# Gated linear attention and a max-of-three feed-forward: a new order of the pieces on five engine queues

## Chip, cores, metric

The kernel runs on one core of a Trainium2 chip. The metric is the device time of one execution in microseconds (us). The engines are TensorE (PE in the profile, its weight loads PEld), VectorE (DVE), ScalarE (ACT), GpSimd (POOL) and SyncE (SP), which here only issues transfers.

## The reference

Two stages, joined by a change of layout. `B, H, S, D = 4, 8, 768, 48`; the second stage has 3072 tokens, model width 384 and hidden width 768.

```python
for t in range(S):
    state = alpha[:, :, t, :, None] * state + einsum('bhd,bhe->bhde', k[:, :, t], v[:, :, t])
    y[:, :, t] = einsum('bhd,bhde->bhe', q[:, :, t], state)
x = y.transpose(0, 2, 1, 3).reshape(B * S, H * D)
h = maximum(maximum(x @ w1, x @ w2), x @ w3)
out = h @ w_out
```

## The kernel before

The recurrence is computed in chunks. A step `s` (0 to 11) is one batch element and 256 tokens; step `s` needs the state that step `s - 4` left. Three weights are needed for one maximum, so the kernel uses max(x w1, x w2, x w3) = x w1 + max(x (w2 - w1), x (w3 - w1), 0): two products per hidden column through `wdif`, and x (w1 w_out) is added in the last product through `w1o`.

Nothing is ordered by loops. `ORDER` is a string of pieces, and `emit` issues them from left to right; each engine runs its own instructions strictly in that order and waits by semaphores for what they need. A piece such as `k0p@5` is letter, index, engine (`v` DVE, `a` ACT, `p` POOL, none for TensorE or SP), step; `#6,4` gives it PSUM banks. One engine's late piece thus holds all its later ones. The letters:

- Loads and stores, all on SP's one queue: `l0` to `l3` load a (alpha), k, q, v of a step into rings of four buffers (L102); `K` loads a third of a weight, part of it into ring buffers of steps 2 and 3 (L118, L121); `J` loads the small constants `ca` and `cb` (L130); `W` stores 128 rows of the output (L500); `D` transposes q and k of a step by DMA (L290), from step 5 on, in two halves.
- Decays: `m` multiplies pairs of alpha (L205); `N` and `r` are logarithms and inverses on ACT (L209, L214, L216); `u` and `w` scale k and q of the nearer token (L219, L222); `c` sums the logarithms on TensorE (L231, L234), one long and four short matmuls; `e`, `f`, `g` are its exponentials on ACT (L240, L250); `k` and `q` scale k and q by them (L260).
- Attention: `T` transposes on TensorE for steps 0 to 4 (L283) and `t` copies the result out; `A` makes scores, 32 small matmuls (L304), and `a` masks them on DVE (L319; L315 for step 0); `V` scales v (L168) and `v` spreads it in two copies; `Y` with even index adds the chunk's part of the output (16 small matmuls, 64 for step 0), with odd index the state's part (12) (L330); `x` copies the result out for the next stage.
- State: `S` makes its update on TensorE (L388), `s` adds it (L400), `M` and `z` decay it (L377, L404), `y` spreads it in two copies.
- Feed-forward: `d` makes the weight differences (L418); `b`, `B`, `n`, `C`, `P`, `p` make `w1o`; `G` is a group of six matmuls of 256 columns (L452), six groups a step; `h` takes the maximum (odd index: always DVE, L461; even: DVE L463 or ACT L465); `O` is the last product (L486), `o` scales it out of PSUM (L168, L170).
- `H` is `warm`: matmuls on a blank tile whose result is not used (L505). `H2^t1@0` waits first for a piece's result (L524). They stand only in the first part.

So a step is: load, decays, `k` and `q`, transposes, `A`, `a`, `Y`, `x`, `G`, `h`, `O`, `o`, `W`; and steps overlap as the string has them.

Of the kernel before, what the change touches and what calls it, by code (L numbers as in the profile page):

```python
# [23 lines left out]
def kernel(  # L24
# [513 lines left out]
    def emit(order):  # L538
# [12 lines left out]
        l0@0 m0v@0 r0a@0 N0a@0 r1a@0 J1@0 l1@0 u0v@0 H15@0#0 c0@0#0 e0a@0 k0v@0 K0@0 b0a@0 f0a@0 J0@0 I0a@0
        H5@0#1 B0@0#1 l2@0 w0v@0 g0a@0 q0v@0 H6@0#2 T0@0#2 M0p@0 l0@1 m0p@1 r0a@1 N0a@1 K2@0 d1v@0 H3@0#3 c0@1#3
        e0a@1 g0a@1 K1@0 d0p@0 r1a@1 T1@0#4 t1v@0 t0a@0 H3@0#5 H2^t1@0#5 A1@0#5,6 l1@1 u0v@1 k0v@1 l2@1 w0v@1
        f0a@1 q0v@1 A0@0#7,0 a0v@0 a2v@0 a1v@0 l3@0 a3v@0 n0a@0 V0a@0 l3@1 V0a@1 v1p@1 v0p@1 K3@0 H5@0#4
        S0@0#4,2 T0@1#3 t0a@1 T1@1#7 t1a@1 H2@0#5 S0@1#5,0 b1a@0 s0v@1 s0a@0 l0@2 m0v@2 N0a@2 K4@0 H1@0#6
        A0@1#6,1 a0v@1 a1v@1 A1@1#3,7 a3v@1 M0p@1 z0p@1 y0a@1 a2v@1 z0p@0 d2p@0 y0a@0 B1@0#5 n1v@0 K5@0 d3v@0
        s1v@0 l0@4 m0v@4 l2@2 c0@2#4 l1@2 g0a@2 M0p@2 Y0@0#6,1 x0a@0 Y3@0 x1a@0 K7@0 K6@0 r0a@2 r1a@2 w0p@2
        Y2@1#7 Y3@1 x1a@1 s1v@1 f0a@2 d4p@0 G1@0#3 N0a@4 l3@2 K8@0 d5p@0 Y0@1#5 u0v@2 e0a@2 q0v@2 G0@0#2 h0a@0
        x0a@1 k0v@2 G2@0#6 G3@0#1 h2a@0 h3v@0 c0@4#7 e0a@4 g0a@4 h1v@0 f0a@4 G2@1#0 h2a@1 G0@1#4 T0@2#2 t0v@2
        T1@2#5 t1v@2 K10@0 l1@4 h0a@1 b2a@0 G1@1#6 h1v@1 K11@0 K9@0 G3@1#1 l0@3 V0a@2 r0a@4 v1a@2 A1@2#3,7 a2v@2  # L560
        A0@2#0,2 a0v@2 a3v@2 S0@2#5,4 s0a@2 a1v@2 B2@0#6 n2v@0 G4@1#3 G4@0#0 G5@1#7 l0@5 z0p@2 l2@4 h3v@1 v0a@2
        Y0@2#5 x0v@2 Y2@2#2 y0a@2 Y3@2 x1a@2 M1p@0 u0p@4 k0v@4 G5@0#6 h4a@0 h5v@0 G5@2#1 l1@3 C2a@0 C0v@0 l2@3
        G4@2#5 l3@3 r1a@4 C1a@0 h4v@2 z1p@0 y1a@0 G0@2#2 m0v@3 s1v@2 h4a@1 G2@2#0 h2v@2 h5v@1 h5v@2 h0a@2 P0@0#6
        P1@0#5 N0a@3 r0a@3 p1a@0 w0v@4 q0v@4 c0@3#4 P2@0#3 e0a@3 m0p@5 G1@2#0 M0p@4 N0a@5 c0@5#7 f0a@3 r0a@5
        r1a@3 p0a@0 u0v@3 k0p@3 p2a@0 G3@2#1 h3v@2 f0a@5 T0@4#2 t0v@4 g0a@5 e0a@5 g0a@3 l3@4 T1@4#5 t1v@4 O0@0#6
        l0@7 l0@6 A1@4#3,1 h1v@2 V0a@3 a2v@4 M0p@5 w0p@3 q0v@3 A0@4#2,7 o0a@0 l1@5 S0@3#4,5 s0a@3 M1p@1 M0v@3
        z0p@3 l1@6 l2@5 O1@0#0 a1v@4 r1a@5 V0a@4 a3v@4 s1v@3 T0@3#3 t0v@3 o1a@0 T1@3#6 t1a@3 z1p@1 O0@1#4 m0p@7
        a0v@4 o0v@1 l0@8 y0a@3 N0a@7 A1@3#7,1 A0@3#5,3 l3@5 v0a@3 S0@4#0,6 W0@0 s0v@4 a1v@3 a0v@3 a2v@3 v0p@4
        m0p@6 N0a@6 O0@2#2 v1a@3 y1a@1 w0v@5 o0a@2 z0p@4 u0p@5 s1v@4 c0@7#4 v1p@4 c0@6#0 O1@1#3 r0a@7 o1a@1
        g0a@7 l0@9 g0a@6 Y3@3#5 a3v@3 Y2@3 Y0@3#7 r0a@8 x0a@3 Y0@4#2 Y2@4#6 l1@7 y0p@4 Y1@4 Y3@4 x1v@4 x0v@4  # L570
        O1@2#3 o1v@2 m0v@8 k0v@5 f0a@6 W1@0 l2@6 G0@4#1 h0v@4 e0a@6 x1a@3 M0p@6 G4@3#7 h4v@3 G2@3#6 G1@3#2
        G3@3#3 h2v@3 h3v@3 G4@4#1 l3@7 W0@2 q0p@5 D0@5 V0a@5 f0a@7 M1p@2 v1a@5 r1a@8 r0a@6 u0p@6 N0a@8 m0p@9
        r1a@6 c0@8#0 G0@3#5 e0a@8 h0a@3 r1a@7 h1v@3 G5@3#7 h5v@3 w0p@6 k0p@6 q0v@6 l3@6 D1@5 G5@4#6 G3@4#3 N0a@9
        V0a@7 h4a@4 h5v@4 e0a@7 c0@9#5 f0a@9 e0a@9 M1p@3 g0a@8 u0p@7 G2@4#2 h2a@4 f0a@8 g0a@9 M0p@8 G1@4#7 h1v@4
        O0@3#1 z1v@2 y1a@2 h3v@4 S0@5#6,4 s0v@5 k0p@7 r0a@9 A0@5#2,0 a1v@5 D1@6 W0@1 D0@6 z0v@5 A1@5#5,7 a2v@5
        a3v@5 o0a@3 V0a@6 l2@7 W0@3 O1@3#3 a0v@5 o1v@3 O1@4#6 y0a@5 o1a@4 r1a@9 v0p@7 v0p@5 Y0@5#0 Y1@5 v0v@6
        s1v@5 x0v@5 Y2@5#5 Y3@5 x1a@5 l0@10 S0@7#7,1 M1p@4 M0p@7 z1p@3 s0v@7 z0p@7 W1@1 l3@8 A1@6#2,3 a2v@6
        a3v@6 A0@6#6,4 a1v@6 S0@6#0,5 s0v@6 G2@5#7 G3@5#2 h2a@5 h3v@5 a0v@6 y0a@7 w0p@7 M1p@5 q0p@7 l1@8 D0@7
        D1@7 l2@8 G4@5#3 h4a@5 G1@5#4 G0@5#0 h0v@5 m0p@10 N0a@10 y1p@3 M0p@9 G5@5#7 O0@4#2 o0a@4 z1p@4 z0p@6
        y0a@6 c0@10#6 e0a@10 f0a@10 h1v@5 h5v@5 O1@5#3 O0@5#0 v1v@7 v1v@6 Y2@6#2 l0@11 s1v@6 u0v@8 k0v@8 g0a@10  # L580
        M1v@6 M0v@10 V0a@8 o1a@5 v0v@8 Y3@6 x1v@6 Y1@6#4 Y0@6 l2@9 r0a@10 S0@8#7 A0@7#5,6 s1v@7 a1v@7 s0v@8
        A1@7#3,2 a3v@7 a0v@7 a2v@7 x0a@6 G2@6#1 h2a@6 G3@6#6 h3v@6 G5@6#7 W1@3 G0@6#2 h0v@6 w0p@8 y1a@4 m0p@11
        z0p@8 N0a@11 W0@4 Y3@7#5 Y2@7 x1v@7 l1@9 W1@2 l3@9 Y0@7#3 Y1@7 x0a@7 c0@11#4 e0a@11 q0p@8 D0@8 D1@8
        g0a@11 r0a@11 w0p@9 M1p@7 l1@10 y0v@8 q0p@9 G1@6#1 h1v@6 G4@6#6 h4a@6 f0a@11 h5v@6 u0v@9 o0a@5 V0a@9
        v0a@9 z1p@5 k0p@9 D0@9 y1a@5 G0@7#2 G5@7#5 G1@7#3 r1a@11 h0v@7 z1p@6 h1v@7 z1p@7 u0p@10 k0p@10 G2@7#1
        G3@7#6 G4@7#4 h4v@7 l3@10 h2v@7 h5v@7 h3v@7 O0@6#7 o0a@6 O1@6#0 D1@9 A0@8#2,3 a0v@8 A1@8#4,1 a2v@8 o1v@6
        a3v@8 v1a@8 V0a@10 S0@9#5 s0v@9 a1v@8 O0@7#6 O1@7#7 v1v@9 z0v@9 Y3@8#2 Y2@8 x1a@8 y0p@9 Y1@8#4 Y0@8
        x0a@8 r1a@10 l2@10 w0p@10 q0p@10 l2@11 w0p@11 S0@10#0 s0v@10 A1@9#1,5 a2v@9 A0@9#3,2 a1v@9 a3v@9 l1@11
        a0v@9 v0a@10 G4@8#4 G0@8#0 h0v@8 G2@8#1 h2v@8 G5@8#2 h4a@8 h5v@8 Y2@9#5 Y0@9#3 l3@11 Y1@9 x0v@9 Y3@9
        y1a@6 G3@8#0 G1@8#1 h3v@8 x1a@9 G0@9#4 h0a@9 u0v@11 G2@9#2 q0v@11 G4@9#3 h1v@8 G5@9#0 D1@10 k0p@11  # L590
        G3@9#5 h2a@9 h3v@9 G1@9#4 D0@10 h4a@9 V0a@11 y1v@7 h5v@9 h1v@9 z0v@10 W1@4 o0a@7 O0@8#1 A0@10#2,5
        A1@10#3,0 a2v@10 a0v@10 a3v@10 D1@11 D0@11 v1v@11 S0@11#4 s0v@11 W0@7 a1v@10 O1@9#6 v1v@10 W1@6 O0@9#3
        o1a@9 W1@9 W0@5 o0a@9 W0@9 A1@11#2,0 a2v@11 a3v@11 A0@11#4,5 W0@6 v0p@11 M0p@11 W1@5 O1@8#6 y0p@10
        Y3@10#3 Y2@10 a0v@11 x1a@10 z0p@11 Y1@10#2 a1v@11 Y0@10 x0a@10 Y1@11#0 y0p@11 Y0@11 x0v@11 Y2@11#4 Y3@11
        o1a@7 W1@7 G3@10#3 x1a@11 G0@10#5 G2@10#2 o0v@8 G1@10#0 h0v@10 G4@10#7 h1v@10 h2a@10 h3v@10 G4@11#4
# [40 lines left out]
```

## Time and profile before

| | |
|---|---|
| runs | 143.85, 144.14, 146.13 us (median 144.14) |
| profiled execution | 143.54 us, its span 141.8 us |
| busy | PE 93%, DVE 80%, ACT 67%, POOL 52% of the span |
| mean granted TensorE clock | 0.988 |
| moved by DMA | 32.42 MB, 229 GB/s on average |
| a load of 384 KB | 5.3 us from issue to landing (median) |
| first, last matmul | 1.19 us; the last begins at 137.99 and ends at 138.3 us |

The span runs from the first to the last instruction; the execution's time is 1.74 us longer. A row of the timeline has start, duration, engine, line, operation and tiles, and in brackets the engine's idle time before it and what ended that. A row of waits has the engine and its line, what it waited for, and total, number and longest. SPq is SP's queue. A row of the table by stages has the stretch, its length, each engine's busy time with its instructions, the granted clock, the DMA engines' share and the rate. Some times in the prediction are of single pieces: the string and the trace were laid side by side, engine by engine. The landing of a transfer is the last of its 16 engines' records.

### The profile page before, as it was taken

How to read it: one execution, taken by the hardware profiler on the slowest of the kernel's cores; microseconds unless marked ns; L12 is line 12 of the kernel's file. 1: busy time of each engine (PE TensorE's matmuls, PEld its weight loads, DVE VectorE, ACT ScalarE, POOL GpSimd, SP SyncE). 2: the span in 40 equal slices, each digit the busy share in tenths (PEclk: the TensorE clock that was granted, in tenths of full speed). 3: DMA queues.
4: the chain of work that ended last, by engine and by line, in shares of the span. 5: the costliest groups of instructions: out<-in, count | busy, mean ns of one | idle time of the engine just before them, and what ended most of it. 6: DMA issues, size and time to landing. Idle time of an engine off the chain costs nothing.

```text
span 141.8 us, 5323 instructions
## 1 busy us (share of the span) xinstructions
PE 132.4 (93%) x2236; PEld 96.6 (68%) x2236; DVE 113.7 (80%) x215; ACT 95.5 (67%) x202; POOL 73.8 (52%) x107
## 2 busy tenths in 40 slices
...
GB/s 107 312 344 325 306 332 269 277 333 361 263 271 249 282 310 253 322 201 109 219 204 274 254 190 332 320 143 182 202 260 199 196 112 161 244 97 16 96 72 150
DMA packets 73031, 32.42 MB, mean 229 GB/s; under 512 B 65456, under 2 KB 73008, under 8 KB 73008
## 3 DMA queue, kind: packets, MB, share of 16 engines
...
q8 instruction: 17, 0.28, 0.8%
...
## 4 chain that ended last, share of the span: by engine, by line
PE 75%; SPq 8%; DVE 7%; DMA 4%; ACT 2%; issue 2%; DVEq 0%
PE bank L452 32%; PE bank L486 23%; PE bank L330 8%; SPq L102 5%; DMA rv<-in_v_dram 4%; PE bank L304 4%; PE bank L388 2%; SPq L118 2%; PE bank L440 2%; PE bank L283 2%; DVE lat L319 1%; DVE hT L461 1%; ACT qkT L162 1%; DVE qk L260 1%; PE bank L231 1%
## 5 line engine op out<-in xcount | busy, mean ns | idle before, releaser
L452 PE MATMUL bank<-xT,wdif 128*128 128x256 f16 x432 | 50.8, 275 | 0.8 <-DVE h L463 0.8
L452 PEld LDWEIGHTS <-wdif 128*128 128x128 f16 x432 | 41.4, 98 | 6.8 <-issue 1.1
L319 DVE TENSOR_TENSOR lat<-bank,cb 128x512 f16<-128x512 f32 x44 | 28.0, 681 | 1.3 <-PE bank L304 1.2
L461 DVE TENSOR_TENSOR hT<-bank,h 128x512 f16<-128x512 f32 x36 | 23.9, 685 | 6.2 <-PE bank L452 3.2
L486 PE MATMUL bank<-wo,hT 128*128 128x384 f16 (+1 forms) x150 | 27.5, 320 | 0.0
L486 PEld LDWEIGHTS <-hT 128*128 128x128 f16 x150 | 14.5, 98 | 8.9
L168 ACT ACTIVATE ob<-bank,ca 128x384 f32<-128x384 f32 (+1 forms) x18 | 10.3, 570 | 14.2 <-PE bank L486 12.9
L465 ACT ACTIVATE h<-bank 128x512 f16<-128x512 f32 x21 | 12.2, 599 | 8.1 <-PE bank L452 7.8
L486 PE MATMUL bank<-w1o,xT 128*128 128x384 f16 (+1 forms) x75 | 15.9, 321 | 0.0
L260 POOL TENSOR_TENSOR qk<-rk,ic 128x768 f16<-128x768 f32 x6 | 11.5, 1920 | 4.7 <-DVE rk L219 3.3
L505 PE MATMUL bank<-hT 128*128 128x512 f16 x42 | 12.7, 440 | 1.4 <-DVE hT L603 1.2
L168 ACT ACTIVATE vt<-rv,ca 128x768 f16<-128x768 f32 x12 | 11.3, 945 | 3.2 <-DMA rv<-in_v_dram 3.2
L162 ACT CAST xT<-bank 128x384 f16<-128x384 f32 x16 | 7.5, 480 | 7.1 <-PE bank L330 7.1
L222 POOL TENSOR_TENSOR rq<-rq,ic 128x384 f32<-128x384 f32 x8 | 8.0, 999 | 7.4 <-DMA rq<-in_q_dram 4.3
L463 DVE TENSOR_SCALAR h<-bank 128x512 f16<-128x512 f32 x15 | 9.9, 680 | 1.2 <-PE bank L452 1.2
L164 POOL COPY vu<-vt 64x384 f16<-64x384 f16 x14 | 7.3, 520 | 5.2 <-ACT vt L168 4.7
L205 POOL TENSOR_TENSOR ra<-ra 128x384 f32<-128x384 f32 x7 | 7.5, 1075 | 3.3 <-DMA ra<-in_alpha_dram 3.2
L162 ACT CAST st<-kept 64x192 f16<-64x192 f32 x26 | 9.0, 347 | 0.3
L260 POOL TENSOR_TENSOR qk<-rq,ac 128x768 f16<-128x768 f32 x5 | 9.1, 1814 | 0.1
L330 PE MATMUL bank<-lat,vu 128*32 128x128 f16 x352 | 8.3, 224 | 0.8 <-issue 0.7
L486 PEld LDWEIGHTS <-xT 128*128 128x128 f16 x75 | 6.5, 98 | 3.1
L505 PEld LDWEIGHTS <-hT 128*128 128x128 f16 x42 | 4.2, 110 | 6.4 <-issue 3.2
...
## 6 DMA issues: line engine op xcount, KB each, us to landing
...
```

Of the source, the lines that this page charges most:

```text
L162: nc.scalar.copy(out=dst, in_=src)
L168: nc.scalar.mul(dst, src, col)
L222: engines[eng].tensor_mul(raw("q", s, 0), raw("q", s, 0), decays["k"][s % 3][:, 0])
L260: engines[eng].tensor_mul(dst, src, by)
L319: nc.vector.tensor_mul(lats[s % 2][u][:, i], bank(("aps", s, u, i), [HP, P]), pmask.unsqueeze(1).broadcast_to([P, HP, P]))
L330: nc.tensor.matmul(y[x][C * m:C * (m + 1), f, :], lhs, rhs, start=(s, x, m) not in begun, stop=(seen[x] or U * (s // B) + x == 0) and n == ...
L452: nc.tensor.matmul(gps[:, j, :], wdif[:, f, g, jj * P:(jj + 1) * P], xT[:, f].rearrange("p u t -> p (u t)"), start=(f == 0), stop=(f == NF ...
L461: nc.vector.tensor_max(hTs[s % NH][:, 2 * jg:2 * jg + 2, :], gps, h)
L463: nc.vector.tensor_scalar_max(h, gps, 0.0)
L465: nc.scalar.activation(out=h, in_=gps, func=AFT.Relu)
L486: nc.tensor.matmul(ops, lhs, (w1o if what == "x" else wo16)[:, j, cols], start=((what, j) == every[0]), stop=((what, j) == every[-1]))
L505: nc.tensor.matmul(wps, blank[:, :P], blank, start=True, stop=True)
```

## The change

Only `ORDER` is replaced. The pieces stay the same but for the `H` fills; their sequence on every engine's queue, the PSUM banks, and the engine of a number of pieces change: `q` on POOL 5 to 9 and on DVE 7 to 3, `u` the same; gates `M` on POOL 17 to 9, on DVE 3 to 11; even `h` on ACT 21 to 26; `o` on ACT 18 to 13, on DVE 7 to 12; one to three pieces each of `b`, `d`, `k`, `m`, `n`, `p`, `s`, `v`, `x`, `y`, `z`, `V`. The transposes stay as they were: steps 0 to 4 on TensorE, 5 to 11 by DMA. The new order comes from a search over a plan whose costs were altered: longer two-part copies (`v`, `y`), dearer small constants (`J`), and TensorE held when a packet of its instructions is asked for late.

The start, the parts around steps 5 and 6, and the end:

```diff
-        l0@0 m0v@0 r0a@0 N0a@0 r1a@0 J1@0 l1@0 u0v@0 H15@0#0 c0@0#0 e0a@0 k0v@0 K0@0 b0a@0 f0a@0 J0@0 I0a@0
-        H5@0#1 B0@0#1 l2@0 w0v@0 g0a@0 q0v@0 H6@0#2 T0@0#2 M0p@0 l0@1 m0p@1 r0a@1 N0a@1 K2@0 d1v@0 H3@0#3 c0@1#3
...
+        K0@0 J0@0 I0a@0 b0v@0 H13@0#0 B0@0#0 l0@0 m0v@0 r0a@0 r1a@0 l0@1 m0v@1 N0a@0 n0v@0 J1@0 H6@0#1 c0@0#1
+        l2@0 w0v@0 f0a@0 q0v@0 e0a@0 r0a@1 N0a@1 g0a@0 M0p@0 H6@0#2 c0@1#2 g0a@1 r1a@1 l1@0 u0v@0 M0v@1 k0v@0
+        H6@0#3 T1@0#3 K2@0 e0a@1 T0@0#4 t0a@0 d1v@0 K1@0 d0v@0 t1v@0 l1@1 u0p@1 l3@1 k0v@1 l2@1 w0v@1 l3@0 f0a@1
+        q0v@1 V0a@1 v1p@1 l0@2 m0p@2 K3@0 K5@0 K4@0 l0@4 l1@2 l2@2 H2@0#5 H1^d0@0#5 A0@0#5,6 a1v@0 A1@0#7,0
+        H1@0#1 S0@1#1,4 s0a@1 v0a@1 V0a@0 K6@0 H5@0#3 T1@1#3 t1a@1 a2v@0 a3v@0 T0@1#2 t0v@1 S0@0#6,1 a0v@0 z0p@1
+        s0a@0 z0p@0 K7@0 s1v@1 d3v@0 N0a@2 K8@0 d2p@0 b1a@0 l3@2 l2@4 l1@4 l0@3 K10@0 K11@0 K9@0 H1@0#3
+        H0^t1@1#3 A1@1#3,7 a2v@1 c0@2#0 e0a@2 y0a@0 g0a@2 Y0@0#2,5 A0@1#6,4 x0a@0 a0v@1 a3v@1 a1v@1 Y3@0 B1@0#3
...
+        s0a@3 z0p@3 y0p@3 M0p@6 A0@3#3,2 z1v@1 Y1@4#1 Y3@4#7 Y2@4 x1a@4 q0p@5 D1@5 D0@5 w0p@6 z1p@2 u0p@6 k0p@6
...
+        h5v@11 O2@11#6 O0@10#7
+        O1@10#4 W0@9 o0a@10 O3@11 W0@10 o0a@11 W0@11 o1v@10 W1@10 O4@11#1,3 O6@11 o2a@11 W2@11 O5@11 o1v@11
+        W1@11
```

More of the change, by code (lines that the diff above doesn't have):

```diff
@@ L550 @@
     ORDER = """
[L551 to L595, printed above, removed]
@@ L596 @@
-        h4a@11 h4a@10 G5@10#1 G2@11#5 h5v@10 o1a@8 W1@8 G3@11#0 h2v@11 h3v@11 W0@8 G0@11#2 h0v@11 G1@11#3 h1v@11
-        G5@11#4 O1@10#7 O2@11#1 o1a@10 W1@10 h5v@11 O0@10#6 o0a@10 O3@11 o0v@11 O4@11#5,0 W0@10 W0@11 O5@11
-        o1a@11 W1@11 O6@11 o2v@11 W2@11
+        K0@0 J0@0 I0a@0 b0v@0 H13@0#0 B0@0#0 l0@0 m0v@0 r0a@0 r1a@0 l0@1 m0v@1 N0a@0 n0v@0 J1@0 H6@0#1 c0@0#1
+        l2@0 w0v@0 f0a@0 q0v@0 e0a@0 r0a@1 N0a@1 g0a@0 M0p@0 H6@0#2 c0@1#2 g0a@1 r1a@1 l1@0 u0v@0 M0v@1 k0v@0
+        H6@0#3 T1@0#3 K2@0 e0a@1 T0@0#4 t0a@0 d1v@0 K1@0 d0v@0 t1v@0 l1@1 u0p@1 l3@1 k0v@1 l2@1 w0v@1 l3@0 f0a@1
@@ new lines @@
+        q0v@1 V0a@1 v1p@1 l0@2 m0p@2 K3@0 K5@0 K4@0 l0@4 l1@2 l2@2 H2@0#5 H1^d0@0#5 A0@0#5,6 a1v@0 A1@0#7,0
+        H1@0#1 S0@1#1,4 s0a@1 v0a@1 V0a@0 K6@0 H5@0#3 T1@1#3 t1a@1 a2v@0 a3v@0 T0@1#2 t0v@1 S0@0#6,1 a0v@0 z0p@1
+        s0a@0 z0p@0 K7@0 s1v@1 d3v@0 N0a@2 K8@0 d2p@0 b1a@0 l3@2 l2@4 l1@4 l0@3 K10@0 K11@0 K9@0 H1@0#3
+        H0^t1@1#3 A1@1#3,7 a2v@1 c0@2#0 e0a@2 y0a@0 g0a@2 Y0@0#2,5 A0@1#6,4 x0a@0 a0v@1 a3v@1 a1v@1 Y3@0 B1@0#3
+        x1a@0 G0@0#2 h0v@0 n1v@0 l0@5 G1@0#6 h1v@0 r0a@2 r1a@2 M0p@2 m0p@4 w0v@2 u0p@2 k0v@2 r0a@4 l3@4 l0@6
@@ new lines @@
+        y0a@1 f0a@2 q0v@2 l2@3 Y2@1#7 G3@0#4 Y3@1 Y0@1#5 N0a@4 x1a@1 x0a@1 G2@0#2 h2a@0 b2v@0 c0@4#3 g0a@4 e0a@4
+        d4p@0 l3@3 G2@1#6 h3v@0 G0@1#0 f0a@4 h0a@1 d5p@0 l1@3 T1@2#7 T0@2#5 t0v@2 t1a@2 B2@0#2 n2v@0 s1v@0 h2a@1
+        G3@1#4 h3v@1 A1@2#3,0 A0@2#5,7 a1v@2 r1a@4 l1@5 w0p@4 G4@1#2 a2v@2 G1@1#1 V0a@2 S0@2#6,4 v0a@2 s0a@2
+        G4@0#7 a3v@2 G5@0#3 v1a@2 a0v@2 Y0@2#6 x0a@2 Y2@2#0 z0p@2 y0v@2 Y3@2 x1a@2 m0v@3 N0a@3 h4a@0 u0v@4 l0@8
+        G5@1#5 M0v@4 k0v@4 G0@2#6 h0a@2 h1v@1 s1v@2 C2a@0 h5v@0 G4@2#0 h4v@2 G2@2#7 c0@3#6 h4v@1 C0a@0 q0p@4
@@ new lines @@
+        h2a@2 f0a@3 C1v@0 G1@2#1 e0a@3 M1p@0 z1p@0 y1a@0 r0a@3 g0a@3 V0a@4 r1a@3 T1@4#4 G3@2#3 h3v@2 t1v@4 m0p@5
+        N0a@5 r0a@5 T0@4#0 G5@2#2 h5v@2 h1v@2 M0v@3 P0@0#7 p0a@0 t0v@4 P1@0#6 h5v@1 p1v@0 P2@0#3 p2a@0 v0p@4
+        v1a@4 m0p@6 N0a@6 c0@5#4 f0a@5 w0v@3 r0a@6 q0p@3 r1a@6 u0p@3 l0@7 S0@4#2,1 A1@4#7,0 A0@4#5,6 a0v@4 a2v@4
+        a3v@4 O0@0#3 o0a@0 l2@5 W0@0 c0@6#5 s0v@4 z0v@4 l3@5 r1a@5 g0a@5 V0a@3 g0a@6 k0v@3 l3@7 e0a@6 u0v@5 l2@6
+        s1v@4 l1@6 l0@9 O0@2#7 o0v@2 O0@1#0 v1p@3 o0a@1 a1v@4 e0a@5 f0a@6 y0a@4 k0p@5 O1@0#3 o1v@0 T0@3#2 t0v@3
@@ new lines @@
+        T1@3#1 O1@1#7 t1a@3 m0v@8 A1@3#0,6 N0a@8 M1v@2 M1v@1 W0@1 S0@3#4,5 o1a@1 v0a@3 m0p@7 N0a@7 a2v@3 w0p@5
+        s0a@3 z0p@3 y0p@3 M0p@6 A0@3#3,2 z1v@1 Y1@4#1 Y3@4#7 Y2@4 x1a@4 q0p@5 D1@5 D0@5 w0p@6 z1p@2 u0p@6 k0p@6
+        Y0@4 x0a@4 r0a@7 q0p@6 a3v@3 a0v@3 l1@7 O1@2#0 l3@6 c0@7#4 g0a@7 f0a@7 e0a@7 G0@4#7 V0a@7 M0p@7 l2@7
+        v1p@7 W0@2 l0@10 u0p@7 k0p@7 y1p@2 s1v@3 r1a@7 w0p@7 M1p@3 z1p@3 o1v@2 c0@8#1 g0a@8 M1p@4 e0a@8 a1v@3
+        G2@4#6 h2a@4 Y3@3#3 D1@6 l0@11 D0@6 r0a@8 q0p@7 z1p@4 m0p@11 Y2@3 x1a@3 V0v@5 v1a@5 l1@8 u0p@8 k0p@8
@@ new lines @@
+        Y0@3#4 l3@8 D1@7 W1@0 G3@4#5 x0v@3 D0@7 l2@8 r0a@9 W1@1 G4@4#0 h3v@4 l3@9 h4a@4 y1v@1 y1p@4 v0p@7 W1@2
+        G1@4#2 m0v@9 r1a@9 h0a@4 r1a@8 w0p@8 G2@3#6 h2v@3 G5@4#3 h5v@4 M0v@8 h1v@4 G1@3#4 G0@3#5 h0a@3 G3@3#0
+        h3v@3 h1v@3 N0a@9 G4@3#7 h4a@3 f0a@8 q0p@8 v0a@5 G5@3#6 h5v@3 S0@5#3,2 A1@5#5,0 a2v@5 a3v@5 M0v@5 s0v@5
+        z0v@5 A0@5#4,7 a1v@5 y0a@5 V0a@6 c0@9#1 s1v@5 a0v@5 e0a@9 l2@9 f0a@9 w0p@9 q0p@9 l1@9 u0p@9 O1@4#6 o1v@4
+        k0p@9 O1@3#5 o1v@3 Y1@5#0 Y3@5#3 Y0@5 Y2@5 g0a@9 D0@8 l1@10 D1@8 m0v@10 N0a@10 M1v@5 r0a@10 u0p@10 z1p@5
@@ new lines @@
+        S0@6#7,2 s0v@6 x1v@5 x0v@5 v0a@6 z0v@6 y0v@6 S0@7#4,6 O0@3#5 s0v@7 c0@10#1 g0a@10 G4@5#7 G0@5#3 h4v@5
+        s1v@6 z0v@7 s1v@7 M1v@6 z1p@6 e0a@10 k0p@10 v1a@6 h0a@5 G2@5#0 G5@5#4 h5v@5 h2a@5 G3@5#7 h3v@5 A0@6#2,6
+        a0v@6 A1@6#3,4 a3v@6 N0a@11 r1a@10 a2v@6 a1v@6 y1p@5 M0p@10 G1@5#0 O0@4#7 h1v@5 c0@11#2 l3@10 W1@4 W1@3
+        y0a@7 M0p@9 Y3@6#4 Y1@6#3 D1@9 D0@9 l2@10 l2@11 w0p@10 f0a@10 q0p@10 o0a@3 V0a@8 W0@3 l1@11 u0p@11 Y2@6
+        x1v@6 e0a@11 g0a@11 M1v@7 Y0@6 x0a@6 S0@8#6 s0v@8 M0v@11 z0v@8 A0@7#0,1 a0v@7 r0a@11 r1a@11 v0v@8 a1v@7
@@ new lines @@
+        A1@7#5,4 a3v@7 a2v@7 f0a@11 w0p@11 q0p@11 O0@5#3 G4@6#6 G2@6#0 G0@6#1 y1v@3 h0v@6 z1p@7 G1@6#4 h1v@6
+        l3@11 o0v@4 W0@4 G3@6#5 Y3@7#2 Y1@7#1 D1@10 Y2@7 Y0@7 D0@10 k0p@11 x1v@7 h4a@6 O1@5#4 h2a@6 y0a@8 x0v@7
+        v1a@8 G0@7#7 G5@6#2 h5v@6 G4@7#6 h3v@6 o0v@5 h0a@7 V0a@9 v0v@9 G2@7#0 h2a@7 G3@7#1 h3v@7 h4a@7 G5@7#2
+        h5v@7 G1@7#5 h1v@7 V0a@10 A0@8#3,7 a1v@8 S0@9#0 s0v@9 A1@8#1,6 a3v@8 a0v@8 O0@6#2 o0a@6 a2v@8 v1v@9
+        z0v@9 v0v@10 O0@7#5 O1@6#7 o0a@7 Y1@8#0 Y0@8 x0v@8 Y3@8#6 Y2@8 x1a@8 W0@6 W0@7 D0@11 D1@11 S0@10#3
```

9 lines of the change are left out of this document (added).

## The prediction

> **What bounds the kernel now.** I read the page first, then the table by stages, then TensorE's waits in the timeline.
>
> ```profile
> span 141.8 us, 5323 instructions
> ...
> PE 132.4 (93%) x2236; PEld 96.6 (68%) x2236; DVE 113.7 (80%) x215; ACT 95.5 (67%) x202; POOL 73.8 (52%) x107
> ...
> q8 instruction: 17, 0.28, 0.8%
> ```
>
> TensorE is the bound. The next tables say when, and what is left to win.
>
> ```profile
> core 0: us, PE busy (x) PEld busy (x) DVE busy (x) ACT busy (x) POOL busy (x), PEclk, DMA share, GB/s
> ...
> 16.00:22.60 6.60, 4.94 (x129) 3.34 (x128) 5.45 (x11) 5.55 (x10) 4.01 (x8) 1.00 1.10 334
> 22.60:26.00 3.40, 3.39 (x109) 2.50 (x108) 3.40 (x7) 3.17 (x9) 1.82 (x3) 0.50 0.91 231
> ...
> 30.00:62.00 32.00, 31.89 (x580) 24.27 (x579) 27.64 (x48) 30.54 (x67) 21.31 (x29) 1.00 1.04 297
> 62.00:90.00 28.00, 27.20 (x527) 20.82 (x527) 26.45 (x52) 20.22 (x46) 18.64 (x28) 1.00 0.97 220
> ```
>
> Up to 22.6 us TensorE waits for data and is filled with `warm` matmuls. In the stretch 22.6 to 26 its granted clock is 0.50. From 30 us on it is almost never idle: an order can win only in the first 30 us, in a few stalls, and in the tail. The stalls:
>
> ```profile
> 21.96 0.32 PE L231 MATMUL bank<-la,ca 128*128 128x384 f16 x1 [0.71 <-ACT la L209]
> 62.93 1.27 DVE L463 TENSOR_SCALAR h<-bank 128x512 f16<-128x512 f32 x2
> 63.66 0.60 PE L452 MATMUL bank<-xT,wdif 128*128 128x256 f16 x4 [0.77 <-DVE h L463]
> 91.00 0.29 PE L330 MATMUL bank<-lat,vu 128*32 128x128 f16 x8 [0.66 <-issue]
> 117.05 0.43 PE L388 MATMUL bank<-vt,qk 64*64 64x48 f16 x16 [0.28 <-DVE hT L461]
> ```
>
> The one at 91.00 waits for no engine ("issue") in the middle of `Y0@7`. The page's queue q8 moves 17 packets of 16,384 bytes; 0.28 MB over 4,472 TensorE instructions is some 64 bytes each, so a packet holds 256 instructions, 128 matmuls with their loads. The DMA records have one packet at 88.44 to 89.36 and TensorE goes on at 91.00: it had run out of instructions.
>
> **The change, part by part.** Apart from the fills (42 `warm` matmuls become 43) the pieces are the same; what moves is their order on five queues and the engine of some copies. From `T0@2` (30.02 us) on, the TensorE work left is the same set of pieces in both orders: before its first `T@2` each has `c@0` to `c@2`, `c0@4`, `G0` to `G3@0`, `G0@1`, `G2@1` and the same T, A, S, Y. So the sum has three terms: when `T@2` starts, the stalls after it, the tail.
>
> *Term 1, the start of `T@2`.* In the changed order K0 and cb load first, a0 and a1 follow. From the landing records, transfers of 384 KB land 1.10 to 1.21 us apart while the queue is full (first at 4.21, twelfth at 15.72). Counted so, the changed list has q1 at 15.4, v0 at 16.6, K5 (sixteenth) at 20.2. Before lost time at places 13 to 15 (1.47, 1.58, 1.94 apart), where `l0@2` waited to be issued until POOL's `d0p` ended at 14.08 in the buffer it loads into. The changed order makes both differences on DVE (0.95 to 1.09 each), done by about 13.5. Half of the loss may stay: K5 at 21.2, bounds 20.2 and 21.9 (before's place 16).
> The rest follows DVE, whose queue runs without a gap: 0.60 a mask or `h` (681 ns of which 80 overlap), 0.88 a `k` or `q`. q1 at 15.4, `w` 0.55, `q` 0.88: 16.8. Three masks 18.6, `t0v@1` 19.2, `a0v@0` 19.8: `Y0@0` starts at 20.0 (before 22.29, where `c0@2` sat in front of it waiting for `la`). Then `y0a@0`, `x0a@0`, `x1a@0` on ACT give `G0@0` at 22.9; TensorE's own work from there to `T1@2` is 4.82: 27.7. DVE from K5: `d3v` 0.95, four masks 2.4, `h0v` 0.6, `n1v` 0.46, `h1v` 0.6, `w` 0.55, `k` 0.88, `q` 0.88, together 7.3: 21.2 + 7.3 = 28.5 (27.7 to 29.2). DVE is later, so **28.5 against 30.02: -1.5**.
> That holds at full clock. Before's clock was halved in 22.6 to 26.0, after a stretch with TensorE 4.94 of 6.6 us busy; G1@0 took 1.36 instead of 0.65. The changed list waits as long in sum, but its `Y0@0` (64 matmuls) and fills stand before 21.3, so I count 2.2 busy us in any 3.4 there, against 1.7 before. If the clock is halved all the same until 26.0, the 3.1 us from 22.9 on do half their work (+1.55) and `T@2` comes at 29.3. Ends: -0.7 to -2.3.
> The Trainium skill, TensorE: Matmul & The Clock Gate, Part 1, says the clock falls to half after about 3.4 us with too little activity, in windows that start anywhere; the half-clock stretch here is 3.41 long, and the trace agrees. By that rule the phase decides, and 29.3 is as possible as 28.5.
>
> *Term 2, stalls after `T@2`.* Before: 0.93 at 62.6, 0.85 at 90.1, 0.44 at 116.6, and 0.27, 0.19, 0.17, 0.17, 0.16 (pitch over the usual one of the piece): 3.2. What goes: the 0.93, where `h0v@4` stood behind `k0v@5`; that `k` took 1.75 instead of 0.98 beside POOL's `m0p@9`, and is on POOL now. The 0.85: counting 128 matmuls from the stall back and forth, before's thinnest packets last 1.75, 2.74, 4.0 and 4.3 us of TensorE time (the one that ran dry 4.3, under a full DMA queue); the changed ones 3.5, 3.8, 4.0, 4.0. The `S0@6` and `Y@5` that made the 1.75 now have `O0@3` behind them. I keep 0.2 of it (0 to 0.85).
> The Trainium skill, Runtime: NRT & Kernel Launch, Instruction fetch mechanics, calls the cost of crossing a 16 KiB block "mostly hidden"; by that no stall would be the packets', and the sum would be 0.65 later. The 0.66 of idle time at 91.00 speaks against it.
> What is late next: `Y3@2` waits for `y0v@2`, put on DVE behind `a0v@2` (two halves of 0.45): 0.45. `S0@2` and `Y2@2` wait for v2, place 24 of the loads: at 31.0 it costs 0.4, at before's 32.4 for that place 1.4, at 30 nothing. `A1@5` needs both transposes of step 5 (below): 0.3. `S0@6` needs v6, queued behind them: 0.2. Others of the size of 116.6: 0.4. With the packets 1.95. **3.2 less 1.95: -1.25**, ends +1.0 and -3.
>
> *Work moved to other engines.* POOL gets four `q` (1.81), four `u` (1.00), one `k` (1.92) and one `y`, and gives up eight gates (0.23), three decays (0.55), a difference (1.82) and an `m` (1.08): +7.6, 81 of some 139. DVE gives those `q` and `u` (0.98, 0.64) and five `h` (0.68) and takes five output scalings (0.61), eight gates, copies and decays: equal within 1 us. ACT loses 2.6. None reaches TensorE; these cost nothing while they lie under its 0.65 a gate group, and where they do not I have put them in term 2.
> *SP.* All loads, transposes and stores stand in one queue, so a waiting `D` holds the loads behind it. Before:
>
> ```profile
> SPq L500 <- ACT ob L168: 15.7, 8, 5.1
> SPq L290 <- POOL gm L377: 4.1, 1, 4.1
> SPq L290 <- POOL rq L222: 4.0, 1, 4.0
> ```
>
> Now `D1@5` waits for `q0p@5`, with k7, v6, q7 and store W0@2 behind it. POOL: `k0p@5` when `e0a@5` is done (50.0), `m`, `w` to 53.9, then `z0p@3` after `s0a@3` (55.4), `y0p@3`, `M0p@6`, `q0p@5`: 55.4 + 0.55 + 0.7 + 0.2 + 1.8 = 58.7. `D0@5` is issued 1.3 later and lands 4.6 after that (D1@5's own row): 64.6. TensorE reaches `A1@5` at about 65.3. Free by 0.7, charged 0.3 above.
> *Term 3, tail.* Before, the last matmul ends at 138.3, then one half-width scaling (0.42), a 96 KB store (1.67 to landing) and the close. The changed order ends with the same three: 0, within 0.5.
>
> **Sum.** -1.5 - 1.25 = -2.75: span 141.75 - 2.75 = 139.0, and with 1.74 around it (143.54 less 141.8) 140.8 us. That execution is 0.4% below the median of the runs (144.14), against which 140.8 is 2.3% faster. A difference under 2%, 141.3 to 147.0, is about what a measurement of this kernel cannot tell from none.
>
> **Rivals.**
> *The start is given back (143.0).* K5 at 21.9 and v2 at 32.4, as at before's places: `T@2` at 29.2 (+0.7), `S0@2` and `Y2@2` +1.0, and the half clock at once, of which DVE's wait hides most (+0.5): 2.2 later than the sum. For it: both orders ask for the same bytes in the first 45 us with the DMA share at 1.0. Against: the wait for `d0p` is gone.
> *Slower: SP held at step 5 (145.2 to 147.4).* POOL now carries k, q and u of most steps. If `q0p@5` comes when before could issue that pair (63.16), `D0@5` goes out at 64.5 and lands at 69.1 to 69.7; `A1@5` starts 4.4 late: 145.2. If POOL stays behind, step 7's pair adds half as much: 147.4. It takes a us for each us past 59.4 at `D1@5`, and before is reached at 62.2. For it: only 0.7 us free, and the longest SPq L290 waits are on POOL. Against: before's own `q0p@5` ended at 59.8, and the 63.16 came from DVE's slow `k0v@5`.
> *The packets are not what the order mends.* If thin packets still run dry once or twice (0.85 each), 141.5 to 142.3: inside the first range.
>
> **How the numbers follow.** Forecast 0.58 (its own range 138.3 to 142.4; 0.08 of it above 141.3), given back 0.20, SP held 0.22 (0.07 at 145, 0.15 above 147). Faster 0.50, same 0.08 + 0.20 + 0.07 = 0.35, slower 0.15. The range runs from the forecast's low end (both first terms at their better ends) to 146.0, which leaves out the upper part of the last case.
>
> **What would show it.** Right: `T1@2` begins at 28 to 29, granted clock 1.0 in 20 to 27 us, no idle time by "issue" over 0.3 inside a Y, no wait over 0.5 at `A1@5`, `D1@5` issued before 60. Term 1 is wrong if `T1@2` begins after 29.5; term 2 if TensorE's idle time after it sums to over 3 us; all of it if a new wait of over 2 us stands at `A1@5`, `S0@2` or `S0@6`.

## The result, and the profile after

The changed kernel takes 154.27 us (median of 6 runs, 153.29 to 157.9) against 143.92 (143.29 to 146.13): ratio 1.0703, 95% interval 1.0658 to 1.0748. Some executions fall in a slower state at a lower granted clock: ratios and intervals, here and below, compare the others alone, while medians and ranges are of all. The profiled execution took 154.09 us, so its span of 152.3 can be laid against before's 141.8. First the page, then the same rows of the table by stages (busy us of PE, PEld, DVE, ACT, POOL, then clock, DMA share, GB/s).

```profile
span 152.3 us, 5343 instructions
...
PE 134.1 (88%) x2236; PEld 96.9 (64%) x2236; DVE 126.8 (83%) x223; ACT 93.0 (61%) x196; POOL 81.4 (53%) x105
```

```profile
16.00:22.60 6.60, 4.40 (x136) 2.95 (x141) 5.43 (x10) 4.66 (x9) 3.17 (x5) 1.00 1.07 323
22.60:26.00 3.40, 3.06 (x109) 2.43 (x86) 3.40 (x6) 3.32 (x10) 2.30 (x3) 1.00 1.01 264
...
30.00:62.00 32.00, 30.65 (x528) 22.80 (x526) 30.50 (x54) 28.52 (x62) 20.73 (x23) 1.00 0.96 262
62.00:90.00 28.00, 25.03 (x452) 18.30 (x453) 27.17 (x44) 20.13 (x45) 24.89 (x28) 0.94 1.15 254
90.00:118.00 28.00, 23.68 (x428) 18.01 (x415) 25.91 (x44) 12.11 (x26) 19.66 (x20) 1.00 0.99 212
```

TensorE works as long as before (134.1 against 132.4) and stands still in the middle: it is busy 25.0 of 28 us in 62 to 90, where before had 27.2, and 23.7 in 90 to 118, where before had 27.0:

```profile
90.00:118.00 28.00, 27.04 (x474) 20.89 (x463) 23.30 (x44) 15.68 (x31) 18.77 (x21) 1.00 0.93 198
```

DVE is full in 62 to 90 (27.2 of 28), with fewer instructions than before (44 against 52). So DVE's instructions took longer. The groups say which (busy us, mean ns of one). Before:

```profile
L319 DVE TENSOR_TENSOR lat<-bank,cb 128x512 f16<-128x512 f32 x44 | 28.0, 681 | 1.3 <-PE bank L304 1.2
...
L164 DVE COPY vu<-vt 64x384 f16<-64x384 f16 x14 | 3.8, 274 | 0.4
L205 DVE TENSOR_TENSOR ra<-ra 128x384 f32<-128x384 f32 x5 | 3.3, 656 | 1.0 <-POOL gm L377 1.0
L164 DVE CAST st<-kept 64x192 f16<-64x192 f32 x4 | 1.8, 446 | 0.0
L404 DVE TENSOR_TENSOR kept<-fa,gm 128x192 f32<-128x192 f32 x3 | 1.4, 467 | 0.0
```

After:

```profile
L319 DVE TENSOR_TENSOR lat<-bank,cb 128x512 f16<-128x512 f32 x44 | 28.0, 680 | 0.9 <-PE bank L304 0.8
...
L164 DVE CAST st<-kept 64x192 f16<-64x192 f32 x8 | 8.5, 1060 | 0.6 <-POOL kept L404 0.4
...
L164 DVE COPY vu<-vt 64x384 f16<-64x384 f16 x8 | 5.6, 701 | 0.1
...
L205 DVE TENSOR_TENSOR ra<-ra 128x384 f32<-128x384 f32 x6 | 5.3, 882 | 2.1 <-DMA ra<-in_alpha_dram 2.1
L404 DVE TENSOR_TENSOR kept<-fa,gm 128x192 f32<-128x192 f32 x6 | 4.8, 807 | 0.1
```

The masks, which read a bank of PSUM, take 680 as ever. What reads SBUF alone has grown: state casts from 446 to 1,060 ns, value copies from 274 to 701. The timeline shows beside what (start, busy us, engine, line; in brackets the idle time before and what ended it):

```profile
35.96 1.81 POOL L260 TENSOR_TENSOR qk<-rq,ac 128x768 f16<-128x768 f32 x1
36.03 2.13 DVE L164 CAST st<-kept 64x192 f16<-64x192 f32 x2 [0.44 <-POOL kept L404]
...
37.93 0.64 PE L330 MATMUL bank<-qkT,st 128*32 128x128 f16 x12 [1.07 <-DVE st L164]
```

```profile
64.79 2.88 DVE L164 CAST st<-kept 64x192 f16<-64x192 f32 x2
65.73 1.81 POOL L260 TENSOR_TENSOR qk<-rk,ic 128x768 f16<-128x768 f32 x1
67.51 1.83 POOL L260 TENSOR_TENSOR qk<-rq,ac 128x768 f16<-128x768 f32 x1
67.70 2.06 DVE L205 TENSOR_TENSOR ra<-ra 128x384 f32<-128x384 f32 x1
...
69.68 0.68 DVE L463 TENSOR_SCALAR h<-bank 128x512 f16<-128x512 f32 x1
...
70.41 0.81 PE L452 MATMUL bank<-xT,wdif 128*128 128x256 f16 x6 [1.28 <-DVE h L463]
```

The two casts of `y0v@2` take 2.13 us instead of 0.90. The first of them takes 1.85 and ends 0.1 us after POOL's `q0p@4` (37.77), the second 0.26; `Y3@2` waits for them. In the second window `y1v@1` and `m0v@9` lie beside POOL's `u`, `k` and `q` of step 6 and take 4.9 us together; the `h` that TensorE needs stands behind them.

I add up, over DVE's instructions without a PSUM operand, what each took over its length with POOL quiet (the median of its form where no POOL instruction overlaps it: 0.26 us for a state cast or a value copy), and call it **the stretch**: 3.9 us in before, **18.9 us** in after. The expectations below say 3.1 and 17.1: they come out, within some tenths, if a cast is counted at 0.45 us, its mean in before, which is stretched itself. TensorE, counted in a like way (the time from the start of one piece to the next over the usual one, after `T@2`), loses 14.7 us instead of 4.3: 10.4 more. `T@2` begins at 30.09 (before 30.02), the tail from the last matmul to the end is 3.5 in both. So the 10.5 us of span are lost in the middle, in stops and in 3.4 us at half clock from 72.80 on (last section).

### The profile page after: what moved, and what is told of

It reads as the page before. It is cut to its first block, busy times and chain, and to the rows that moved or that the text cites. A ratio compares the mean times of both kernels' runs of the same rounds, so it can differ in the third digit from the quotient of the medians.

```text
span 152.3 us, 5343 instructions
## 1 busy us (share of the span) xinstructions
PE 134.1 (88%) x2236; PEld 96.9 (64%) x2236; DVE 126.8 (83%) x223; ACT 93.0 (61%) x196; POOL 81.4 (53%) x105
## 4 chain that ended last, share of the span: by engine, by line
PE 49%; DVE 22%; DMA 12%; issue 5%; SPq 5%; ACT 3%; POOL 2%; POOLq 0%; DVEq 0%; ACTq 0%
PE bank L486 21%; PE bank L452 16%; DMA rv<-in_v_dram 4%; DMA ra<-in_moe_w_dram 4%; PE bank L330 4%; DVE hT L461 4%; DMA rk<-in_k_dram 3%; DVE vu L164 3%; DVE lat L319 3%; PE bank L304 3%; DVE st L164 3%; PE bank L440 2%; SPq L130 2%; SPq L118 2%; DVE ra L205 1%
## 5 line engine op out<-in xcount | busy, mean ns | idle before, releaser
L465 ACT ACTIVATE h<-bank 128x512 f16<-128x512 f32 x26 | 15.2, 595 | 15.0 <-PE bank L452 14.1
L486 PEld LDWEIGHTS <-hT 128*128 128x128 f16 x150 | 14.8, 100 | 9.6 <-issue 1.0
L260 POOL TENSOR_TENSOR qk<-rq,ac 128x768 f16<-128x768 f32 x9 | 16.4, 1822 | 1.0 <-DVE rq L222 0.7
L168 ACT ACTIVATE ob<-bank,ca 128x384 f32<-128x384 f32 (+1 forms) x13 | 7.3, 569 | 12.2 <-PE bank L486 12.2
L304 PE MATMUL bank<-qkT 48*64 48x128 f16 x384 | 10.2, 224 | 2.8 <-DVE xT L164 1.7
L170 DVE TENSOR_SCALAR ob<-bank,ca 128x384 f32<-128x384 f32 (+1 forms) x12 | 7.1, 595 | 5.2 <-PE bank L486 5.2
L162 ACT COPY vu<-vt 64x384 f16<-64x384 f16 x22 | 11.2, 508 | 0.3
L219 POOL TENSOR_TENSOR rk<-rk,ra 128x384 f32<-128x384 f32 x9 | 9.0, 997 | 4.0 <-DMA rk<-in_k_dram 4.0
L404 POOL TENSOR_TENSOR kept<-fa,gm 128x192 f32<-128x192 f32 x6 | 3.0, 506 | 15.1 <-DVE fa L400 14.2
L304 PEld LDWEIGHTS <-qkT 48*64 48x64 f16 x384 | 6.9, 108 | 5.8 <-issue 4.3
```

Source lines behind the costliest of these rows:

```text
L162: nc.scalar.copy(out=dst, in_=src)
L168: nc.scalar.mul(dst, src, col)
L219: engines[eng].tensor_mul(raw("k", s, 0), raw("k", s, 0), raw("a", s, 1))
L260: engines[eng].tensor_mul(dst, src, by)
L304: nc.tensor.matmul(aps[i][to * J:(to + 1) * J, a * U + n, :], qkT[rows, r, 1, p, cols], qkT[rows, :, 0, p, cols], start=True, stop=True)
L465: nc.scalar.activation(out=h, in_=gps, func=AFT.Relu)
```

## The experiments

Theory: a DVE instruction on SBUF operands can't go on while a POOL instruction runs; the change puts SBUF-only pieces of DVE beside POOL's 1.8 us multiplications, and TensorE waits for what stands behind them. Rivals: the sequence itself (a piece in the wrong place of an in-order queue), or simply more work on POOL and DVE.

**Both halves of the change alone.** `ORDER` of after with the engine that before has for each piece (three of them are shown), and the reverse:

```diff
- y0v@2 ... q0p@4 ... y1v@1 ...
+ y0a@2 ... q0v@4 ... y1a@1 ...
```

> The changed order, every piece on the engine that it had before. Theory (DVE held by POOL): in the changed kernel DVE's instructions with both ends in SBUF take 17.1 us longer than such instructions alone, against 3.1 before, because they wait for POOL's long k and q; with before's engines this falls to 3 to 6 us and the time to 143 to 148. Rival (the order itself: bank order, later loads): 151 to 155, as the sequence is untouched. Rival (POOL too full, transposes late): the time falls as well, but DVE's stretch is not what falls.

> Before's order, every piece on the engine that the change gives it. Theory (DVE held by POOL): the copies and gates that move to DVE meet POOL's long k and q here too; DVE's stretch rises from 3.1 us to 8 or more and the time to 148 to 156. Rival (the order itself): within 2% of before, 141 to 147, as the sequence is before's.

195.74 us (ratio 1.338, 1.319 to 1.357) and 170.61 (1.177, 1.168 to 1.186). Both miss, and so does the stretch of the first, which is 13.5 us and not 3 to 6; the second has 10.0, where 8 or more was expected. The order is worked out for its engines: swapped wholesale, pieces stand in queues behind others that wait. In the first, one wait of DVE for a load is 11.9 us long. These two tell nothing between the theories.

**Nine copies from DVE to ACT.** The nine pieces that lie beside POOL's long ones, in their places:

```diff
- y0v@2 y1v@1 y0v@6 y1v@3 v0v@8 v1v@9 v0v@9 v0v@10 V0v@5
+ y0a@2 y1a@1 y0a@6 y1a@3 v0a@8 v1a@9 v0a@9 v0a@10 V0a@5
```

> The changed kernel with nine of DVE's pieces moved to ACT: y0@2, y1@1, y0@6, y1@3, v0@8, v1@9, v0@9, v0@10, V0@5. POOL's work is untouched. They cost DVE 15.8 us in the changed kernel, 9.1 of them stretch. Theory (DVE held by POOL): TensorE's stops at Y3@2, G5@3, G0@6, Y1@7 and A1@9 (about 8 us together) shrink to under 3 us, the time falls to 147 to 150. Rival (POOL too full, transposes late): no change, 153 to 155. Rival (the order itself): at most 1 us less.

147.37 us (ratio 1.0145, 1.004 to 1.025), 6.9 less than after, as the theory has it. The stretch falls from 18.9 to 10.2, and TensorE's loss from 14.7 to 7.2. But DVE also lost the work of nine copies, so the rival of sheer work is not out.

**The price by itself.** A kernel that stores zeros and computes nothing of the reference: each of ten forms of DVE instruction six times alone, then beside a row of sixty of POOL's 128x768 multiplications.

```diff
+        dve_forms(6)
...
+        pool_busy(60)
+        dve_forms(6)
```

> A kernel of its own, which computes nothing of the reference and stores zeros: ten forms of DVE instruction, six each, first with the other engines idle, then beside an unbroken row of POOL's q multiplications (128x768, 1.8 us each), then beside an unbroken row of ACT copies. Theory (DVE held by POOL): beside POOL the forms with only SBUF operands (state cast, value copy, value scaling, m, gate, z) take up to 1.8 us or 3.6 us apart, two to ten times their time alone; the forms that read PSUM (masks, maximum, state addition, x copy) keep their 0.35 to 0.68 us; beside ACT all are as alone. Rival (SBUF bandwidth in general): all forms stretch a little, beside ACT too. Rival (the stretch is in the queue or semaphores of the real kernel): no form stretches here.

DVE's groups, first in the part beside POOL, then in one with POOL idle:

```profile
L404 DVE TENSOR_TENSOR kept<-fa,gm 128x192 f32<-128x192 f32 x6 | 11.1, 1846 | 0.2
L164 DVE COPY vu<-vt 64x384 f16<-64x384 f16 x5 | 9.1, 1824 | 0.2
...
L568 DVE TENSOR_TENSOR hT<-bank,h 128x512 f16<-128x512 f32 x6 | 4.1, 690 | 0.2
L565 DVE TENSOR_TENSOR lat<-bank,cb 128x512 f16<-128x512 f32 x6 | 4.1, 689 | 0.2
```

```profile
L568 DVE TENSOR_TENSOR hT<-bank,h 128x512 f16<-128x512 f32 x6 | 4.1, 690 | 0.2
...
L404 DVE TENSOR_TENSOR kept<-fa,gm 128x192 f32<-128x192 f32 x6 | 2.1, 358 | 0.2
L164 DVE CAST st<-kept 64x192 f16<-64x192 f32 x6 | 1.5, 251 | 0.2
L164 DVE COPY vu<-vt 64x384 f16<-64x384 f16 x6 | 1.5, 251 | 0.2
```

A copy of 251 ns takes 1,824 on average, a decay of 358 takes 1,846: one DVE instruction for each POOL instruction of 1,802, however short its own work. The smallest form, a gate of 164 ns, gets two through: 1,656 and 166 by turns. The forms that read PSUM don't move at all (690 and 690, and two smaller ones at 357 and 557). This is not shared bandwidth, where a longer instruction would lose more: forms of 557 and 621 ns took about 2,040. Beside these two POOL lost as well, 1,997 instead of 1,802. The part of this run that was to lie beside ACT told nothing, since ACT's row had ended at 157.8 and DVE came to it at 166.

**More off DVE, beyond the nine.** Six gates and two multiplications more go to POOL, and `b2v@0` ahead of `q0v@2`:

```diff
- M0v@4 M1v@2 M0v@8 M1v@5 M1v@6 M0v@11 m0v@3 m0v@10
+ M0p@4 M1p@2 M0p@8 M1p@5 M1p@6 M0p@11 m0p@3 m0p@10
```

> The kernel with the nine pieces on ACT, in which DVE still loses 10.2 us beside POOL: six gates and m0@3 and m0@10 go to POOL as well, and b2v@0 is moved ahead of q0v@2, out of the way of POOL's d4 and d5. Theory (DVE held by POOL): of the 10.2 us some 6 go, POOL gets 3.4 us more, the time falls from 147.4 to 144 to 146. Rival (what is left of the slowdown is the order itself): 147 or more.

168.06 us (1.163, 1.157 to 1.169): the stretch fell as expected, from 10.2 to 4.7, and the time missed: 144 to 146 was expected. The waits say why:

```profile
ACT la L209 <- POOL ra L205: 21.8, 2, 21.3
PE bank L231 <- ACT la L209: 21.5, 4, 20.2
POOL rq L222 <- DMA rq<-in_q_dram: 14.4, 5, 10.6
```

`m0p@10` stood in POOL's queue behind pieces that wait for loads, and `c0@10` waited 20 us for it. One misplaced piece made most of the miss; but before that wait, too, the order was 1.0 us behind the nine alone (`O0@3` at 78.8 against 77.8) and 0.9 ahead of after, so the smaller stretch brought nothing there.

**Before, with the nine on DVE.**

```diff
- y0a@2 y1a@1 y0a@6 y1p@3 v0a@9 v0a@10 V0a@5
+ y0v@2 y1v@1 y0v@6 y1v@3 v0v@9 v0v@10 V0v@5
```

> Before's order and engines, only the same nine pieces put on DVE (six of them were on ACT, one on POOL, two on DVE already). Theory (DVE held by POOL): they take 5.6 us of DVE alone and 2 to 5 us of stretch where POOL runs k, q or u beside them; the time rises by 1 to 5 us. Rival (only the sequence matters): within 1% of before. Rival (DVE simply too full, no stretch): the same rise with no instruction longer than alone.

Two of the nine (`v0@8`, `v1@9`) are on DVE in before already, so seven move. 156.01 us (1.071, 1.065 to 1.077). Slower, as the theory says, but by 7.1%, some 10 us, where 1 to 5 was expected and the stretch rose by 6.5 (3.9 to 10.4). The copies' own work on DVE and new waits in that order come on top, so the size is not explained by the stretch alone, and a DVE that is simply too full is not out by this run.

**POOL's long ones to DVE.** Eight of POOL's key and query multiplications, most of them beside stretched copies, go to DVE:

```diff
- q0p@4 q0p@5 k0p@6 q0p@6 k0p@8 q0p@9 k0p@11 q0p@11
+ q0v@4 q0v@5 k0v@6 q0v@6 k0v@8 q0v@9 k0v@11 q0v@11
```

> The changed kernel with its nine DVE pieces left where they are; instead the eight POOL multiplications of 1.8 us that ran beside them (q0 of steps 4, 5, 6, 9, 11 and k0 of 6, 8, 11) go to DVE. DVE gets 7.6 us more of its own work. Theory (DVE held by POOL): its stretch falls from 17.1 to under 9 us, so DVE's busy time stays about 126 and the time is 149 to 154. Rival (DVE has too much work to do, no interference): DVE's busy time rises to 134 and the time to 158 or more.

180.04 us (1.237, 1.224 to 1.251). The stretch fell to 8.3 and DVE's busy time from 126.8 to 123.4 although it took eight pieces on: right. The time missed the 149 to 154 and lies where the rival had it (158 or more), though not for the rival's reason, a DVE busy for 134 us. DVE now stands in its queue until POOL has the `u` and `w` that those pieces read.

```profile
DVE qk L260 <- POOL rk L219: 15.6, 3, 9.8
```

**What of POOL holds DVE.** Again a kernel that stores zeros: two DVE forms beside short and long POOL instructions, then ten forms beside ACT.

> A kernel of its own, which computes nothing of the reference and stores zeros: DVE's state cast and z, five each, beside unbroken rows of POOL's value copy (64x384, 0.52 us), m (128x384, 1.0), gate (128x4, 0.2) and memset, and last all ten forms beside a row of ACT casts. Theory (DVE held by POOL): each DVE instruction waits for the POOL instruction that runs, so it takes about the length of one of POOL's (0.5, 1.0, 0.25) plus its own 0.25 to 0.36; beside ACT every form is as alone. Rival (only the 1.8 us multiplications hold DVE): 0.25 and 0.36 beside the short ones. Rival (any SBUF traffic): longer beside ACT too.

The cast (251 alone) and the decay (358 alone) took 528 and 540 beside POOL's value copies (509 each), about 1,030 beside its 128x384 multiplications (992), and 252 and 358 beside its gates and memsets (210 and 214), apart from one cast in each row (482 and 621), which overlaps the POOL copy of 0.50 ahead of the row. Beside ACT's casts all ten forms took what they take alone. So the price goes by the length of the POOL instruction that is running, and ACT has no part in it.

**Nothing moved, POOL's instructions cut in four.** The test that changes neither order, nor engine, nor queue:

```diff
+        if eng == "p":
+            for r in range(R):
+                for h in range(0, H, H // 2):
+                    part = (slice(None), r, slice(h, h + H // 2))
+                    nc.gpsimd.tensor_mul(dst[part], src[part], by[part])
+            return
         engines[eng].tensor_mul(dst, src, by)
```

> The changed kernel with its order, its engines and its queues as they are; alone POOL's sixteen multiplications of keys and queries (128x768, 1.81 us each) are each written as four of 128x192. By the row of POOL's state gate (128x192, 0.51 us) four take about 2.0 us, so POOL is 3 us busier in all. If DVE's copies wait for the POOL instruction that is running, they now wait a quarter of it: DVE's stretch falls from 17.1 us to 5 to 8, the state casts from 1.06 us to 0.5 to 0.6, and the time falls from 154.3 to 146 to 151 us. Rival, that the sequence itself or an engine's queue makes the 10 us: no instruction has changed its place, so the time stays at 153 to 156.

> The same four pieces in the version with nine copies on ACT (147.4 us, stretch 10.2). If stretch is what is left there too, it falls to 4 to 6 us and the time to 143 to 146; if that version's rest is its sequence, 147 to 148.

> The same four pieces in the kernel before, whose DVE has only 3.1 us of stretch, 0.8 of it in one key multiplication that ends a stop of TensorE of 0.9 us (that one lies beside a multiplication of POOL that is not split). Both theories: 143 to 145 us; the extra 3 us on POOL lie beside other work. A time below 142.5 would say that before's own stretch costs more than its stops show.

**147.82 us** (ratio to before 1.0226, 1.0164 to 1.0288), 6.5 less than after, although POOL is busier. The page and the groups of this version:

```profile
PE 133.4 (92%) x2236; PEld 97.2 (67%) x2236; DVE 117.1 (81%) x223; ACT 92.7 (64%) x196; POOL 90.7 (62%) x153
```

```profile
L164 DVE CAST st<-kept 64x192 f16<-64x192 f32 x8 | 3.5, 438 | 0.1
...
L410 DVE TENSOR_TENSOR kept<-fa,gm 128x192 f32<-128x192 f32 x6 | 3.0, 504 | 0.4 <-POOL gm L383 0.4
...
L164 DVE COPY vu<-vt 64x384 f16<-64x384 f16 x8 | 2.7, 338 | 0.1
```

```profile
L264 POOL TENSOR_TENSOR qk<-rq,ac 128x192 f16<-128x192 f32 x36 | 21.0, 614 | 1.6 <-DVE rq L222 1.3
```

The same 223 DVE instructions take 117.1 us instead of 126.8; the casts are back at 438, about before's 446, if not at their 0.26 alone. The stretch is 9.3 instead of 18.9 (some 7.5 as the expectation counts), TensorE's loss 7.1 instead of 14.7. The stops before `G5@3` (1.44), before `G0@6` (1.60) and at `A1@9` (2.02) are gone. A quarter takes 614 ns, not the 510 expected, so POOL rose by 9.3 us and not by 3; one wait of TensorE for it shows, 0.55 us in `S0@7`. For the 6.5 us neither the sequence nor sheer work can be the cause: the one is as in after, the other more.

With the nine copies on ACT as well it is 146.83 us (1.0186, 1.0136 to 1.0236), where 143 to 146 was expected: the stretch is 5.0, near before's 3.9, but TensorE still loses 7.2. The two cures don't add, and what is left over before is mostly not stretch there: two losses that show are before `Y2@2` to `G5@1` (1.6) and before `G4@3` (0.96, ended by an `h` on ACT). In quarters alone one stop is still of the old kind: `b2v@0` takes 2.18 us instead of 0.50 beside POOL's weight differences, which were not cut, and TensorE waits 0.73 us for it before `B2@0`. No run settled these 3 us. Before in quarters is 143.50 us (0.9966, 0.9932 to 1.0000), as good as before and no more; no version here beats it clearly.

**The start.** In the version in quarters:

```diff
- K0@0 J0@0 I0a@0 ... n0v@0 J1@0 H6@0#1
+ K0@0 J0@0 J1@0 I0a@0 ... n0v@0 H6@0#1
```

> The version in quarters (147.8 us), with one DMA moved: the small constants J1 are issued directly behind J0 and not between a1 and k0. In the changed kernel J1 took 2.08 us to issue, l1@0 landed 1.81 us after the load ahead of it instead of 1.15, and K5 landed at 22.46 against 21.2 forecast. If J1's place costs that, l1@0 lands 0.4 to 0.7 earlier, and with it K1, q1 and K5 (22.45 to about 21.9); T1@2 (30.67 there) comes up to 0.5 earlier and the time is 147.0 to 147.8. Rival: the small constants cost the queue the same wherever they stand, or the loss is made up again before K5, where l0@2 lands 2.3 us after the load ahead of it: K5 stays at 22.3 to 22.6 and the time at 147.5 to 148.2.

148.33 us (1.0275, 1.0154 to 1.0396). Four runs from 147.01 to 150.29 don't tell the two apart; K5 does, for the rival. `l1@0` landed 0.3 earlier (10.40), the gain was gone at `l0@2`, 2.8 us behind the load ahead of it, and K5 came at 22.58. What makes `l0@2` late (2.3 in after, 2.8 here) was found in small part only: SP had issued the load ahead of it by 13.90 and sent it at 14.29, just after the end (14.26) of `d0v@0`, which reads the buffer that `l0@2` loads into; in after these two times are 14.10 and 14.01. `T1@2` came 0.56 earlier (30.11), but the clock was not halved at the start here, as it was in the version in quarters.

## Why the prediction was wrong

**The step that failed** is "Work moved to other engines": "DVE equal within 1 us ... None reaches TensorE; these cost nothing". POOL's part was right (81.4 against 81). DVE's was not: its copies were priced by their rows in before (0.45 a half of `y0v@2`), where few of them met a long POOL instruction. DVE's own work did stay nearly equal (126.8 less 18.9 against 113.7 less 3.9); but beside POOL's 1.8 us multiplications, of which this order has sixteen instead of eleven, the pieces wait for the POOL instruction to end: 18.9 us of stretch instead of 3.9. DVE was already near full in 30 to 90 us, so it had little room to hide that. Term 2 therefore counted 1.95 us of stops where TensorE lost 14.7. The cut in quarters takes 9.6 us of stretch away and 6.5 to 7.1 of the time with no piece moved, so two thirds of the 10.4 are shown to be this; for the other 3 us or so the cause stays open.

The warning stood in before's own trace, and in the text on record: `k0v@5` "took 1.75 instead of 0.98 beside POOL's `m0p@9`". I read it as one stall that goes away and not as a price for every SBUF-only piece. The Trainium skill, SBUF — State Buffer, section "SBUF: two separate sides", says it outright: VectorE and GpSimd share a pair of ports under an exclusive lock, which goes for a whole instruction to whichever starts first, a GpSimd instruction or a VectorE one that has two SBUF inputs or runs in a two-port mode; the other blocks fully, while TensorE and ScalarE never wait. The runs agree: 251 ns became 1,845 beside a POOL instruction of 1,802, 690 stayed 690 where one operand was in PSUM, and nothing moved beside ACT.

**Term 1, the start** (28.5 forecast, 30.09 measured). DVE's chain was right: 7.6 us from K5 to `T1@2`, 7.3 forecast. K5 was not: 22.46, past the bound of 21.9. I had one recovered delay in the queue, that of `l0@2`, and read it wrongly: in before `d0p@0` ended at 14.07, but SP was still issuing the load ahead until 14.45 and sent `l0@2` at 14.63, so `d0p@0` was not what held it. In after it is no earlier behind that load, and others came beside it: `l0@0` 2.06 us behind the load ahead, `l1@0` 1.81, `l3@0` 1.58 and `l0@2` 2.32. a2 at 20.31 instead of 17.8 held `c0@2`, and `Y0@0` behind it began at 22.41 instead of 20.0. The rival "the start is given back" was right on this part.

**The clock at the start** came as forecast, 1.00 in 16 to 26 us against 0.50 in before, but by luck: in quarters, with the same order, it is halved from 22.45 to 25.86.

```profile
22.60:26.00 3.40, 3.40 (x104) 2.57 (x86) 3.39 (x5) 3.22 (x10) 2.35 (x3) 0.52 1.00 257
```

It gained nothing, since data was late. **The packets** came as forecast too: no idle time by "issue" over 0.3 us inside a Y is left. That the order did it is not shown: before in quarters has before's order, and there too no two matmuls of its `Y0@7` start more than 0.12 us apart. The packet that the prediction names had landed at 89.36, 1 us before the stop in before began (90.34). A term of 0.65 us is invisible beside a missing one of 10.

**SP at step 5.** `D1@5` was issued at 62.98, not 60, and `D0@5` landed at 68.95, but `A1@5` began at 71.93: TensorE was later than the data, so SP wasn't the holder. The rival with SP forecast the right direction, for a reason that didn't come. **The tail** was right: 0.
